# Seventh product of a unit added into the bank that VectorE has just read, instead of into a copy of it

## The chip, the cores and the metric

The kernel runs on one core of one Trainium2 chip. The metric is the device time of one execution in microseconds; lower is better.

## The reference

The reference mixes two results per token with a gate: an attention with a compressive memory over four segments, and a gated feed-forward network. The change lies in the feed-forward half; S = 2048 tokens, D = 576, F = 4608.

```
def _B_ref(x, w_gate, w_up, w_down):
    g = _silu(x @ w_gate)
    u = x @ w_up
    return (g * u) @ w_down
x = A_x
g = sigmoid((x * gate_w).sum(-1, keepdims=True))
a = _A_ref(x, A_wq, A_wk, A_wv, A_wo, A_beta)     # 32 heads, softmax within 4 segments of 512, memory M, z between them
b = _B_ref(x, B_w_gate, B_w_up, B_w_down)
return g * a + (1 - g) * b
```

## The kernel before, in words

The program has three stretches. The first makes the projections of the attention. The last makes the output projection and mixes. Between them, from about 222 to 1634 us, lies the long stretch in which the feed-forward network is computed and the attention runs in its gaps. The change is in this stretch.

**Units.** The 2048 tokens are taken in two halves of 1024, and the 4608 inner features in 36 blocks of 128, so there are 72 units. A unit computes, for one block f and one half, two blocks of 512 tokens of both `x @ w_gate` and `x @ w_up`. That is a product of 2x2 blocks, and it is done with seven block products instead of eight (the sums of weights and of tokens that it needs are made ahead of time). Each operand is split into a high and a low part, so a block product, `seven(t, j)`, is seven matmuls of 128 x 512 into one PSUM bank: six at L1018 and a last one at L1021, which takes the remaining 64 rows of D. With `first=False` a product is added to what the bank holds already.

**The order in a unit** is written out by hand. In it, `a`, `xx` and `y` are PSUM banks (0, 1 and 2), `p5`, `sg0` and `sg1` are rows in SBUF. Products are counted 0 to 6.

| line | engine | what it does |
|---|---|---|
| L1079 | TensorE | product 0 into `a` |
| L1080 | ScalarE | copy of `a` into `xx` |
| L1082, L1083 | TensorE, ScalarE | product 1 into `y`, copied to `p5` |
| L1085, L1087 | TensorE, VectorE | product 2 added in `a`; `y = a + p5` |
| L1089, L1090 | TensorE, ScalarE | product 3 added in `xx`, copied to `sg0` |
| L1092 | TensorE | product 4 added in `a` |
| L1094 | ScalarE | copy of `a` into `xx` |
| L1095 | VectorE | `p5 = a + p5` |
| L1097 | ScalarE | silu of `sg0` |
| L1098, L1099 | TensorE, ScalarE | product 5 added in `y`, silu of it to `sg1` |
| L1102 | TensorE | product 6 added in `xx` |
| L1103, L1104 | VectorE | `sg0 = xx * sg0`, `sg1 = p5 * sg1` |

**What runs between the products.** After each product stands a `tick()`, which calls `beat`. It starts whatever is due by a list of delayed steps: ScalarE's high parts and VectorE's low parts of the next unit's weights (L268, L271), of this unit's results (L962, L963; in some units L136, L137), GpSimd's sums, loads and stores. It then puts groups of the down product (nine matmuls of L868, summed by VectorE at L878) in place, two or three at each tick from the third on, if there are any. Groups come due once in three units, in the unit that follows a full set of three blocks. Then it may advance the attention by a step. A step can hold score matmuls (L726), VectorE's row minimum of the masked scores (L732), ScalarE's exponential (L744), VectorE's and GpSimd's split of it (L758, L759) and the product with the values (L774, L775, summed by VectorE at L781). In units without groups the attention rests at the three ticks after product 5 and 6, so that product 6 follows product 5 directly.

All engines work through their queues in the order in which these lines are issued. The order of accesses to a PSUM bank is kept by semaphores, which the framework sets by tile; all uses of a bank number are uses of one tile.

The bank of a tile is chosen where the helper is made:

```
a_tile = banks(0)
x_tile = banks(1)
y_tile = banks(2)
```

Of the kernel before, what the change touches and what calls it, by code (L numbers as in the profile page):

```python
# [16 lines left out]
AF = mybir.ActivationFunctionType  # L17
# [49 lines left out]
def gated_mix(ctx, tc, xT, xrest, wf, wfr, wfh, wd, wv, wo, beta, cmask, ident, bmask, out):  # L67
    nc = tc.nc
# [31 lines left out]
    def banks(*ids):  # L100
        turn = cycle(ids)
        return lambda shape=(P, L): ps.tile(list(shape), F32, name=f"bank{next(turn)}")
# [4 lines left out]
    first_tile = banks(0, 1, 2, 3, 4)  # L107
    lone_tile = banks(7)
    v_tile = banks(5, 6, 7, 4, 0, 5, 6, 7, *8 * (5, 6, 7))
    a_tile = banks(0)  # L110
    x_tile = banks(1)
    y_tile = banks(2)
    taken = {}
    clock = [0]
# [120 lines left out]
    def r_block(h, o):  # L235
        i, c = divmod(h, 2)
        a, t = (rp.tile([P, 7, 64], d, name=z, bufs=1) for d, z in ((F32, "rr"), (F32R, "rt")))

        def sums():
            nc.gpsimd.tensor_sub(a[:, 5], a[:, 0], a[:, 1])  # L240
            nc.gpsimd.tensor_add(a[:, 1], a[:, 1], a[:, 3])
            nc.gpsimd.tensor_sub(a[:, 4], a[:, 1], a[:, 0])
            nc.gpsimd.tensor_sub(a[:, 6], a[:, 2], a[:, 4])

        def keep(k):
            d = rc[i, 32 * k:32 * k + 32].rearrange("r f (j n) -> (r f) j n", n=P)
            nc.sync.dma_start(d[:, :, 64 * c:64 * c + 64], f32(t))

        return [(o, lambda: nc.sync.dma_start(a[:, 0:4], wfh[h - 4])), (o + 2, sums),
                (o + 3, lambda: nc.scalar.activation(t, a, AF.Copy)), (o + 3, lambda: keep(0)), (o + 3, lambda: keep(1)),  # L250
                (o + 4, lambda: nc.vector.tensor_sub(t, a, f32(t))), (o + 5, lambda: keep(2))]

    def r_fetch(f):
        nc.sync.dma_start(f32(rhs[f % 2][:96]).rearrange("p j n -> p (j n)"), rc[f // 4, :, f % 4])
# [33 lines left out]
    with ExitStack() as st:  # L288
# [188 lines left out]
        for kt in range(NT):  # L477
            if kt % 2 == 0:
                both = staging(), staging()
            a = both[0][:, L * (kt % 2):L * (kt % 2) + 3 * P].rearrange("p (m n) -> p m n", n=P)  # L480
# [209 lines left out]
    with ExitStack() as st:  # L690
# [12 lines left out]
        def row_tile():  # L703
            return rw.tile([P, L], F32, name="row")

        def w_fetch(f):
            ops = wops[1, f] = [None] * 7

            def one(j):
                ops[j] = op_tile()  # L710
                nc.sync.dma_start(f32(ops[j]).rearrange("p a k n -> p (a k n)"), wc[f, j])

            return [(j + 2 if f else FIRST[j], lambda j=j: one(j)) for j in range(7)]
# [219 lines left out]
        def c_tr(o, me):  # L933
            if me is not None:
                nc.gpsimd.tensor_add(o[:, 0:D], o[:, 0:D], me)
            nc.gpsimd.tensor_copy(o[:, 576:640], o[:, 512:576])
            ta = half_tile([P, 4, P])
            for k in range(4):
                nc.tensor.transpose(ta[:, k], o[:, P * k:P * k + P], idt)
            tb = lone_tile([P, P])  # L940
            nc.tensor.transpose(tb, o[:, 512:640], idt)
            oh = cps[0].tile([P, 4, P], F32R, name="oh")
            ol = cps[0].tile([P, 4, P], F32R, name="ol")
            os_ = cps[0].tile([P, P], F32R, name="os")
            split(oh, ol, ta)
            xs_split(os_, tb)
            r = []
            for k in range(4):
                r += [oh[:, k], ol[:, k], oh[:, k]]
            return r + [os_, os_]  # L950
# [31 lines left out]
        def feed(half, f):  # L982
            return [(f // CH, i, hf, hs, ds, yas[half], half) for i in range(8) for hf in range(2)]
# [29 lines left out]
        def seven(t, j, first=True):  # L1013
            w, x = ops[j], XO[j]
            n = 0
            for z in range(2):
                for p, q in ((0, 0), (0, 1), (1, 0)):
                    nc.tensor.matmul(t, w[:, p, z], x[z][:, q], start=first and n == 0, stop=False,  # L1018
                                     skip_group_check=True)
                    n += 1  # L1020
            nc.tensor.matmul(t, rem[:, RPOS[j]], XR[j], start=False, stop=True, skip_group_check=True)  # L1021
# [7 lines left out]
        for pos, (half, f) in enumerate(seq):  # L1029
            if f == 0:  # L1030
                yas[half] = yp.tile([P, 8, D], F32, name="ya")
            q = f % CH
            nxt = seq[pos + 1] if pos + 1 < len(seq) else None
            if q == 0 and f:
                groups += feed(half, f - 1)
                fed.append(f)
            plan = []
            if not nxt:
                plan.append((3, lambda: early.append(c_tr(*tiles.pop(0)))))
            if nxt:  # L1040
                plan += w_fetch(nxt[1]) if nxt[0] and nxt[1] < KEPT else w_make(*nxt)
                if nxt != (0, 1):
                    plan.append((1 if nxt[1] else 10, lambda f=nxt[1]: r_fetch(f)))
                for n, h in enumerate(BLOCKS.get(pos, ())):
                    plan += r_block(h, 4 * n)
                if f + 2 < FT:
                    wraw_of[f + 2] = [None, None]
                    for u in range(2):
                        plan.append(((2, 5)[u] if f or not half else 5 + u, lambda u=u, f=f: wraw_of[f + 2].__setitem__(u, w_load(f + 2, u))))
            if pos == FT - 2:  # L1050
                X2, XR2 = [[None, None] for _ in range(7)], [None] * 7
                plan += [(o + 8, fn) for o, fn in x_second(X2, XR2)]
            for o, fn in plan:
                defer(o + 1, fn)
            step = [0]

            def tick():
                k = step[0]
                step[0] += 1
                if k % 2 == 0 and f and stores:  # L1060
                    nc.sync.dma_start(*stores.pop(0))
                if half == 0:
                    if (q, k) in ((0, 3), (1, 3), (2, 2)):
                        draw[f] = d_load(f)
                    if (q, k) in ((1, 1), (1, 7), (2, 4)):
                        g = f - 1 if k == 1 else f
                        ds[half, g] = d_split(g, draw.pop(g))
                elif (q, k) in ((1, 0), (1, 2), (2, 1)):
                    g = f - 1 if k == 0 else f
                    ds[half, g] = d_fetch(g)  # L1070
                beat(k, half)

            ops, rem = wops.pop((half, f)), rhs[f % 2]
            hh = fp.tile([P, 2, L], F32R, name="hh")
            hl = fp.tile([P, 2, L], F32R, name="hl")
            hs[half, f] = hh, hl
            a, y, xx = a_tile(), y_tile(), x_tile()
            p5, sg0, sg1 = (row_tile() for _ in range(3))
            seven(a, 0)  # L1079
            nc.scalar.activation(xx, a, AF.Copy)  # L1080
            tick()
            seven(y, 1)  # L1082
            nc.scalar.activation(p5, y, AF.Copy)  # L1083
            tick()
            seven(a, 2, False)  # L1085
            y = y_tile()
            nc.vector.tensor_add(y, a, p5)  # L1087
            tick()
            seven(xx, 3, False)  # L1089
            nc.scalar.activation(sg0, xx, AF.Copy)  # L1090
            tick()
            seven(a, 4, False)  # L1092
            xx = x_tile()
            nc.scalar.activation(xx, a, AF.Copy)  # L1094
            nc.vector.tensor_add(p5, a, p5)  # L1095
            tick()
            nc.scalar.activation(sg0, sg0, AF.Silu)  # L1097
            seven(y, 5, False)  # L1098
            nc.scalar.activation(sg1, y, AF.Silu)  # L1099
            tick()  # L1100
            tick()
            seven(xx, 6, False)  # L1102
            nc.vector.tensor_mul(sg0, xx, sg0)  # L1103
            nc.vector.tensor_mul(sg1, p5, sg1)  # L1104
            if q == CH - 1:
                defer(2, lambda t=(hh[:, 0], hl[:, 0], sg0): split(*t))
            else:
                split_by(2, hh[:, 0], hl[:, 0], sg0)
            split_by(3, hh[:, 1], hl[:, 1], sg1)
            tick()  # L1110
            assert not groups
            if f == FT - 1:
                groups += feed(half, f)
                if half == 0:
                    for n in range(BREAK):
                        beat(None if n > 1 else n)
                        if n == 0:
                            down_parts([groups.pop(0) for _ in range(3)], CH - 1, CH)
                    XO, XR = X2, XR2
                    assert not groups  # L1120
# [98 lines left out]
```

## Time and profile before

| | us |
|---|---|
| median of 3 runs | 1725.83 |
| lowest, highest | 1724.3, 1725.91 |
| the profiled execution, its own time | 1724.43 |
| its span | 1722.7 |

| engine | busy, us | instructions |
|---|---|---|
| TensorE, matmul | 1706.5 | 11868 |
| VectorE | 1359.8 | 3231 |
| ScalarE | 1084.8 | 2123 |
| GpSimd | 938.4 | 1194 |

A row of the timeline gives the start, the duration, the engine, the line, the operation, what is written and read, and how often; in brackets how long the engine stood idle before it, and what ended that. A row of waits reads: who waited, for whom, us in total, times, longest. A row of groups gives the count, the busy time and the mean ns of one, then the idle time of the engine just before such instructions and what ended it. PE is TensorE's matmul, PEld its loading of weights, DVE is VectorE, ACT ScalarE, POOL GpSimd, SP the queue that issues transfers.

### The profile page before, as it was taken

Reading aid. Unit: us, or ns where it says so; the run is one execution under the profiler, and the core shown is the slowest. Engines: PE = TensorE matmul, PEld = TensorE weight load, DVE = VectorE, ACT = ScalarE, POOL = GpSimd, SP = SyncE. Lnnn points to the kernel's source line nnn. Section 1 sums busy time; section 2 is a strip of 40 time slices with the busy share of each in tenths; the row PEclk is TensorE's granted clock in tenths of the full one; section 3 lists DMA queues with packets and bytes.
Section 4 is the critical chain, followed back from the end, with each engine's and each line's share of the span. In section 5 each row is a group of like instructions: output and inputs, shape, how many; then the busy total and the mean of one; then the engine's idle time right before and its main releaser. Section 6 shows DMA issues by size and latency. Waiting matters only on the chain.

```text
span 1722.7 us, 34832 instructions
## 1 busy us (share of the span) xinstructions
PE 1706.5 (99%) x11868; PEld 1481.0 (86%) x11868; DVE 1359.8 (79%) x3231; ACT 1084.8 (63%) x2123; POOL 938.4 (54%) x1194
## 2 busy tenths in 40 slices
PE   9999999999999999999999999999999999999999
PEld 7899978888888888888887888888888888888899
DVE  6557588898899889898989677788887778778655
ACT  7666585776677577667765755765666576566411
POOL 4434646666666656565666555555555555555221
PEclk9999999999999999999999999999999999999999
DMA  8654499999998898988879986887778677767544
GB/s 284 233 186 153 151 311 191 232 226 186 209 227 192 181 215 200 193 198 203 210 144 256 290 177 133 178 186 162 148 181 182 147 157 185 163 132 167 165 144 137
DMA packets 524002, 328.05 MB, mean 190 GB/s; under 512 B 411184, under 2 KB 460336, under 8 KB 523824
## 3 DMA queue, kind: packets, MB, share of 16 engines
q1 hardware_dynamic: 523824, 325.83, 77.5%
q8 instruction: 93, 1.52, 0.4%
q14 instruction: 85, 0.70, 0.1%
HBM read 165.76 MB, written 76.09 MB: 140 GB/s over the span
## 4 chain that ended last, share of the span: by engine, by line
PE 83%; DVE 6%; ACT 5%; DMA 3%; issue 2%; POOL 1%; SPq 1%; DVEq 0%; ACTq 0%; POOLq 0%
PE bank L1018 33%; PE bank L868 24%; PE bank L159 10%; PE bank L1021 5%; PE bank L726 4%; PE bank L774 2%; PE bank L775 1%; PE bank L414 1%; ACT pe L744 1%; ACT L744 1%; PE bank L460 1%; DVE xo L137 1%; DVE p L758 1%; DVE scr L732 1%; PE bank L350 1%
## 5 line engine op out<-in xcount | busy, mean ns | idle before, releaser
L759 POOL TENSOR_TENSOR p<-pe,p 128x512 f16<-128x512 f32 x320 | 376.0, 1175 | 420.4 <-DVE p L758 406.2
L868 PE MATMUL bank<-dw,hh 128*128 128x320 f32 (+1 forms) x2304 | 489.0, 305 | 2.8 <-DVE ya L878 2.8
L868 PEld LDWEIGHTS bank<-dw,hh 128*128 128x128 f32 x2304 | 381.4, 190 | 14.4 <-DVE ya L878 3.8
L744 ACT ACTIVATE pe<-bank,mb 128x512 f32<-128x512 f32 (+3 forms) x512 | 247.9, 526 | 197.7 <-DVE mb L732 191.3
L868 PE MATMUL bank<-dw,hl 128*128 128x320 f32 (+1 forms) x1152 | 340.6, 296 | 0.2 <-DVE hl L137 0.2
L732 DVE CUSTOM_DVE_ANT_0 scr<-bank,cm 128x512 bf16<-128x512 f32 (+3 forms) x512 | 246.6, 482 | 6.8 <-PE bank L726 0.2
L878 DVE TENSOR_TENSOR ya<-bank,ya 128x320 f32<-128x320 f32 x352 | 158.3, 453 | 83.9 <-PE bank L868 83.2
L868 PEld LDWEIGHTS bank<-dw,hl 128*128 128x128 f32 x1152 | 218.0, 189 | 0.4 <-DVE hl L137 0.4
L1021 PE MATMUL bank<-xr,rh 128*128 128x512 f32 x504 | 196.5, 390 | 0.0
L752 POOL TENSOR_SCALAR_AFFINE_SELECT pe<-pe 128x256 f32<-128x256 f32 (+1 forms) x320 | 149.8, 469 | 54.1 <-ACT pe L744 51.0
L758 DVE CAST p<-pe 128x512 f16<-128x512 f32 x320 | 152.5, 477 | 0.0
L264 POOL TENSOR_TENSOR ws<-raw 128x256 f32<-128x256 f32 x140 | 118.3, 845 | 17.4 <-DMA raw<-in_wf_dram 4.5
L726 PE MATMUL bank<-kst,qst 108*128 108x512 bf16 (+3 forms) x512 | 125.2, 306 | 2.1 <-ACT pe L744 2.1
L1021 PEld LDWEIGHTS bank<-xr,rh 128*128 128x128 f32 x504 | 94.7, 188 | 20.3
L963 DVE TENSOR_TENSOR hl<-row,hh 128x512 fp32r<-128x512 f32 x120 | 104.2, 868 | 8.3 <-ACT hh L962 7.8
L1095 DVE TENSOR_TENSOR row<-bank,row 128x512 f32<-128x512 f32 x72 | 49.7, 690 | 64.7 <-ACT bank L1094 64.5
L744 ACT ACT_TABLE_LOAD x69 | 88.5, 1283 | 11.1 <-DVE mb L732 10.1
L1080 ACT ACTIVATE bank<-bank 128x512 f32<-128x512 f32 x72 | 41.9, 582 | 80.5 <-PE bank L1021 77.4
L1090 ACT ACTIVATE row<-bank 128x512 f32<-128x512 f32 x72 | 43.3, 601 | 78.0 <-PE bank L1021 77.8
L1097 ACT ACT_TABLE_LOAD x71 | 91.1, 1283 | 1.3
L264 POOL TENSOR_TENSOR ws<-raw,ws 128x256 f32<-128x256 f32 x70 | 58.3, 833 | 49.4 <-DVE wo__22504 L271 10.9
L159 PE MATMUL bank<-xo,qhi 128*128 128x512 f32 x264 | 83.2, 396 | 0.4 <-ACT vps L399 0.4
(2166 smaller groups left out, 4097.9 us busy)
## 6 DMA issues: line engine op xcount, KB each, us to landing
raw<-in_wf_dram SPq DMA_DIRECT2D x140, 256.0 KB
rh<-rc SPq DMA_DIRECT2D x72, 336.0 KB
dc<-dw SPq DMA_DIRECT2D x36, 576.0 KB
dw<-dc SPq DMA_DIRECT2D x36, 576.0 KB
stk<-q SPq DMA_DIRECT2D x32, 384.0 KB
draw<-in_wd_dram SPq DMA_DIRECT2D x36, 288.0 KB
rc<-rt SPq DMA_DIRECT2D x42, 224.0 KB
vd<-vps SPq DMA_DIRECT2D x8, 912.0 KB
```

What stands on the lines that cost most here:

```text
L159: nc.tensor.matmul(t, st[n], mv[n], start=(n == 0), stop=(n == 13))
L264: (nc.gpsimd.tensor_sub if sub else nc.gpsimd.tensor_add)(src[j], p(), q())
L726: nc.tensor.matmul(t[:, c:c + w], qs[:KR, pr, P * i:P * i + P], ks[:KR, pr, 0:w], start=True, stop=True)
L732: nc.vector.tensor_tensor_reduce(scr[:, :w], t[:, c:c + w], cm[:, L - w:L], -SCALE, 3.0e38, OP.add, OP.min, m[:, k:k + 1])
L744: nc.scalar.activation(pe[:, c:c + w], t[:, c:c + w], AF.Exp, bias=m[:, k:k + 1], scale=SCALE)
L752: nc.gpsimd.affine_select(d, d, pattern=pat, compare_op=OP.is_ge, fill=0.0, base=0, channel_multiplier=1)
L758: nc.vector.tensor_copy(p[:, 0], pe)
L759: nc.gpsimd.tensor_sub(p[:, 1], pe, p[:, 0])
L868: nc.tensor.matmul(ts[m], p, q[:, cs], start=(n == 0), stop=(n == 3 * CH - 1))
L878: nc.vector.tensor_add(ya[:, i, cs], t, ya[:, i, cs])
L1018: nc.tensor.matmul(t, w[:, p, z], x[z][:, q], start=first and n == 0, stop=False, skip_group_check=True)
L1021: nc.tensor.matmul(t, rem[:, RPOS[j]], XR[j], start=False, stop=True, skip_group_check=True)
```

## The change

Product 6 is added in `a`, the bank that holds the sum of products 0, 2 and 4, after VectorE has read it at L1095. The copy of that bank by ScalarE (L1094) is gone, and L1103 reads `a` instead of `xx`. Since `a` is now in use until the end of the unit, the two banks change places by unit: the helper gives banks 0, 1, 1, 0, 0, 1, 1, 0 and so on, so that `a` is bank 0 and `xx` bank 1 in one unit, and the other way round in the next.

```
-    a_tile = banks(0)
-    x_tile = banks(1)
+    ax_tile = banks(0, 1, 1, 0)
...
-            a, y, xx = a_tile(), y_tile(), x_tile()
+            a, y, xx = ax_tile(), y_tile(), ax_tile()
...
             seven(a, 4, False)
-            xx = x_tile()
-            nc.scalar.activation(xx, a, AF.Copy)
             nc.vector.tensor_add(p5, a, p5)
             tick()
             nc.scalar.activation(sg0, sg0, AF.Silu)
...
             nc.scalar.activation(sg1, y, AF.Silu)
             tick()
             tick()
-            seven(xx, 6, False)
-            nc.vector.tensor_mul(sg0, xx, sg0)
+            seven(a, 6, False)
+            nc.vector.tensor_mul(sg0, a, sg0)
             nc.vector.tensor_mul(sg1, p5, sg1)
```

## The prediction

> **What bounds the kernel now.** I read the page first: who is busy, and is there anything to win on the busiest engine?
>
> ```profile
> span 1722.7 us, 34832 instructions
> PE 1706.5 (99%) x11868; PEld 1481.0 (86%) x11868; DVE 1359.8 (79%) x3231; ACT 1084.8 (63%) x2123; POOL 938.4 (54%) x1194
> ```
>
> TensorE is filled to 99%; no matmul is added or removed. So the change can only move the moments in which TensorE stands still. The view of waits says which these are, and the rows of VectorE and ScalarE say who waits around the edited lines:
>
> ```profile
> PE bank L1018 <- ACT bank L1094: 3.6, 6, 1.4
> PE bank L868 <- DVE ya L878: 2.8, 4, 0.9
> PE bank L726 <- ACT pe L744: 2.1, 6, 0.4
> PE bank L1018 <- DVE bank L1087: 1.1, 2, 0.7
> PEld bank L1018 <- ACT bank L1094: 8.0, 11, 1.9
> DVE row L1095 <- ACT bank L1094: 64.5, 57, 2.8
> DVE row L1103 <- PE bank L1021: 25.4, 40, 1.9
> DVE row L1103 <- ACT row L1097: 3.1, 5, 0.9
> DVE bank L1087 <- PE bank L1021: 12.5, 21, 1.6
> DVE bank L1087 <- ACT row L1083: 11.4, 12, 1.8
> ACT bank L1094 <- PE bank L1021: 64.0, 44, 3.3
> ```
>
> The columns are total us, times, longest. TensorE's largest wait is exactly for the copy that the change deletes (L1094, first row; the weight loader's row, 8.0, is its upper bound). But the sixth row warns: VectorE's sum L1095, which becomes the new releaser of the seventh product, today starts after that copy, 57 times of 72. Rows of groups by form give the sizes (the third is for a rival further down):
>
> ```profile
> L1094 ACT ACTIVATE bank<-bank 128x512 f32<-128x512 f32 x72 | 42.2, 587 | 64.4 <-PE bank L1021 64.0
> L1095 DVE TENSOR_TENSOR row<-bank,row 128x512 f32<-128x512 f32 x72 | 49.7, 690 | 64.7 <-ACT bank L1094 64.5
> L758 DVE CAST p<-pe 128x512 f16<-128x512 f32 x320 | 152.5, 477 | 0.0
> ```
>
> **The change, part by part.** *Removed: 72 copies of 587 ns, 42.2 us of ScalarE.* ScalarE is idle 37% of the span and stood idle 64.0 us in front of this very copy, so its 42.2 us bring TensorE nothing by themselves. What comes back is the stall in front of the seventh product. I count the products 0 to 6, as the code does: the result of product 4 is copied (L1094) and summed (L1095), product 5 lies between, and product 6 waits. Each product is six matmuls of L1018 and one of L1021. Its stall is the distance from the start of product 5's last matmul to the start of product 6's first one, less the 0.23 us by which such matmuls follow each other when nothing stops them (844.55 to 844.78 in the second of these timelines). The first unit shows a stall; the first two rows are the last matmuls of products 4 and 5:
>
> ```profile
> 229.08 0.39 PE L1021 MATMUL bank<-xr,rh 128*128 128x512 f32 x1
> 230.67 0.39 PE L1021 MATMUL bank<-xr,rh 128*128 128x512 f32 x1
> 231.87 0.50 PE L1018 MATMUL bank<-xo,wo__2681 128*128 128x512 f32 x1 [0.81 <-ACT bank L1094]
> 231.24 0.58 ACT L1094 ACTIVATE bank<-bank 128x512 f32<-128x512 f32 x1
> 230.03 0.08 DVE L732 DVE_READ_ACCUMULATOR2_ANT mb<- 128x1 f32 x1
> 231.85 0.69 DVE L1095 TENSOR_TENSOR row<-bank,row 128x512 f32<-128x512 f32 x1 [1.74 <-ACT bank L1094]
> ```
>
> Stall: 231.87 - 230.67 - 0.23 = 0.97 us; the copy ended at 231.82 and the matmul started 0.05 later. Done for all 72 units from the same rows, the stall shows in ten units: 0.97, 0.49, 0.06, 0.55, 0.23, 0.50, 0.21, 0.51, 0.05 and 1.60, together **5.2 us**. That all goes.
>
> *Added: product 6 waits for L1095.* Its matmuls now write the bank that L1095 reads. Behind the waiting matmul TensorE has product 6, the down products, the attention steps and the next unit in its queue, and VectorE's own L1103 waits for product 6; so the wait is paid in full. So the question is when L1095 would end without the copy ahead of it: as soon as product 4 is done and VectorE is through with what is queued before it, plus 0.69. In the first unit VectorE was through at 230.11 and product 4 ended at 229.47 (229.08 + 0.39), so L1095 would end by about 230.8, before TensorE is ready at 230.90: the 0.97 is won there. It is otherwise where VectorE is the late one:
>
> ```profile
> 844.55 0.39 PE L1021 MATMUL bank<-xr,rh 128*128 128x512 f32 x1
> 844.78 0.39 PE L1018 MATMUL bank<-xo,wo__11789 128*128 128x512 f32 x1
> 843.43 0.58 ACT L1094 ACTIVATE bank<-bank 128x512 f32<-128x512 f32 x1 [1.76 <-PE bank L1021]
> 842.32 1.39 DVE L758 CAST p<-pe 128x512 f16<-128x512 f32 x1
> 843.63 0.62 DVE L781 TENSOR_REDUCE acc<-bank 128x152 f32<-128x456 f32 x1
> 844.17 0.68 DVE L732 CUSTOM_DVE_ANT_0 scr<-bank,cm 128x512 bf16<-128x512 f32 x1
> 844.78 0.68 DVE L1095 TENSOR_TENSOR row<-bank,row 128x512 f32<-128x512 f32 x1
> ```
>
> Here the copy was done at 844.01 and TensorE went on at 844.78 without a pause; VectorE, without one idle moment, got to L1095 only at 844.78 and ended it at 845.46. With the change TensorE waits for it: 845.46 + 0.05 - 844.78 = 0.73 us, out of nothing. The first and the last unit of this kind:
>
> ```profile
> 243.67 0.39 PE L1021 MATMUL bank<-xr,rh 128*128 128x512 f32 x1
> 244.39 0.50 PE L1018 MATMUL bank<-xo,wo__2816 128*128 128x512 f32 x1 [0.33 <-ACT bank L1094]
> 244.37 0.69 DVE L1095 TENSOR_TENSOR row<-bank,row 128x512 f32<-128x512 f32 x1
> ...
> 1628.65 0.39 PE L1021 MATMUL bank<-xr,rh 128*128 128x512 f32 x1
> 1630.47 1.65 PE L1018 MATMUL bank<-xo,wo__22927 128*128 128x512 f32 x6 [1.43 <-ACT bank L1094]
> 1630.52 0.29 DVE L171 TENSOR_TENSOR os<-bank,os 64x128 fp32r<-64x128 f32 x1
> 1630.84 0.69 DVE L1095 TENSOR_TENSOR row<-bank,row 128x512 f32<-128x512 f32 x1
> ```
>
> 243.67 + 0.23 = 243.90 is when TensorE is ready; L1095 ends at 245.06; 245.06 + 0.05 - 243.90 = 1.2 us instead of 0.49. In the last unit 1631.53 + 0.05 - 1628.88 = 2.7 instead of 1.60. Where L1095 had waited for the copy I put its end at 0.61 after the end of VectorE's instruction before it (such instructions overlap by some 0.08, as at 844.78). Over the 72 units fifteen have a stall: 1.22, 0.41, 0.58, 1.07, 0.50, 0.28, 0.87, 0.26, 0.12, 0.13, 0.59, 0.73, 0.12, 0.50, 2.71, together **10.1 us**. All fifteen are units in which no groups of down products are due, so that only product 5, 1.6 us (229.08 to 230.67), separates product 4 from product 6. In the 22 units with such groups whole groups of nine matmuls stand between, and none of them stalls.
>
> *Is L1095 really free of the copy?* Both only read the bank, so no data goes from one to the other; the 57 waits are there because two engines are kept off one bank. The Trainium skill's page PSUM — Partial Sum Buffer, section "PSUM bank collisions raise a hardware error", says so: accesses of different engines to one bank must be ordered, reads against reads too. By that rule the order disappears with the copy, as I reckon, and the trace agrees with its 64.5 us. If the wait came from something that stays, L1095 would keep its present end: product 6 would then stall in 34 units for 18.0 us by the same working, 12.8 more than now. I take 10.1 because nothing in the code but the copy orders the two.
>
> *What is moved: the banks change places.* The first product of the next unit goes to the bank that L1090 read last, some three products earlier, instead of the one that L1095 read; neither is awaited in any row of TensorE above. ScalarE's copy L1080 overwrites the bank that L1103 reads, as before. I cost this at nothing; its cover is the two or three products of 1.6 us each between; without it each unit would stall by a read of 0.6 us. No DMA and no queue of SP or GpSimd is passed.
>
> *Relief.* VectorE loses 64.5 us of waiting. For TensorE that counts only if it lasts until L1095 of the next unit. It mostly doesn't: VectorE falls back into step with TensorE at L1103 (40 of 72) and at L1087 (33 of 72 by the two rows). Where it runs through, three or four units, 0.1 to 0.6 us each can be saved; I take 0.5 us in all, with 0 and 1.2 as the bounds. The other three TensorE rows (2.8, 2.1, 1.1) hang on L878, L744 and L1087, which lie elsewhere in the unit; I leave them.
>
> **Sum:** -5.2 + 10.1 - 0.5 = +4.4 us. The profiled execution took 1724.43 us (span 1722.7 and 1.7 around it): 1728.8. Two of the three timed runs lie at 1725.8 and 1725.9, so the median, 1725.83, is 1.4 above the profiled one; I forecast **1730.2 us** for the median. A measurement of this kernel tells about 0.2% (3.5 us) from no change; 4.4 us is 0.25%.
>
> **Rivals.** *Faster: VectorE's freed time carries over.* The mean wait that goes is 64.5 / 57 = 1.13 us. If VectorE reached L1095 1.1 us earlier in the fifteen units, only the last one and a trace of the second would be left of the list, 1.7 us; the balance is -3.5, about 1722.3, and with all stalls gone 1720.6. From 0.4 us on it breaks even (the list less 0.4 each leaves 5.2). For it: without the copy ScalarE reaches the gate's L1097 earlier, for which L1103 waits 3.1 us, 5 times. Against it stands the falling into step named above. A unit with 1.07 us in the list shows how:
>
> ```profile
> 431.76 0.70 DVE L1087 TENSOR_TENSOR bank<-bank,row 128x512 f32<-128x512 f32 x1 [0.50 <-ACT row L1083]
> ```
>
> VectorE was idle at L1087, so whatever it had gained before is lost there; what makes it late comes after, in the same unit, and doesn't move. Chance 0.16.
>
> *No change that shows.* The same mechanism at about half strength: VectorE 0.2 to 0.5 us earlier leaves 7.3 to 4.3 us of stalls, -0.9 to +2.1 us, 1725 to 1728. For it: the forecast lies close to the bound. Chance 0.22.
>
> *Far slower: VectorE becomes the bound of these units.* Its instructions stretch (the cast at 842.32 took 1.39 us where its mean is 477 ns) when other engines shift. If it came one operation of 0.69 us later in each unit without groups, the fifteen stalls would grow by 10.4 and those units that are now less than 0.7 us early would add some 3.5: about +18 us, 1744. Or the order against the copy has another cause: +12.8, 1738. Against both: the rows around L1095 don't depend on the copy. Chance 0.10.
>
> **How the numbers follow.** The forecast, 0.52: stalls between 8 and 13 us, 1727.5 to 1734; nine tenths of it lie over 0.2%. Slower: 0.52 x 0.9 + 0.10 = 0.57, with the upper edge of the middle case 0.60. Same 0.24. Faster 0.16. The range reaches down into the faster case, to 1722, and up to the unfavourable order, 1737; the ends of the two outer cases are left out.
>
> **What would show it.** In the changed profile TensorE's row "L1018 <- ACT L1094" must be gone and a row that names VectorE's sum of L1095 stand in its place, with 10 to 16 waits, the longest in the last unit; VectorE's 64.5 us must be gone, and its idle time at L1103 larger. ScalarE must have 72 ACTIVATEs and 42 us less. The first unit must be faster by about a microsecond and the unit at 844 slower by 0.7. I am wrong if the new row is under 5 us (VectorE gained more than I gave it) or if a new wait stands at product 0 or at L1080 (the exchange of banks).

## The result and the profile after

The changed kernel takes 1730.44 us (median of 7 runs, 1729.02 to 1733.13) against 1725.05 (7 runs, 1724.3 to 1725.91). The ratio is 1.0032, with a 95% interval of 1.0022 to 1.0041: slower by 5.4 us. Lines behind the edit move up by one to three: the seven products are L1017 and L1020 now, VectorE's sum is L1092, its product L1100.

The first lines of the page and the rows of waits that answer to those shown before (who waited, for whom, us in total, times, longest):

```profile
span 1728.7 us, 34789 instructions
PE 1707.4 (99%) x11868; PEld 1480.9 (86%) x11868; DVE 1362.6 (79%) x3231; ACT 1048.8 (61%) x2051; POOL 939.7 (54%) x1194
```

```profile
PE bank L1017 <- DVE row L1092: 7.5, 10, 2.1
PE bank L867 <- DVE ya L877: 2.8, 4, 0.9
PE bank L725 <- ACT pe L743: 2.1, 6, 0.4
PE bank L1017 <- DVE bank L1086: 0.7, 1, 0.7
...
DVE row L1100 <- PE bank L1020: 40.3, 48, 2.6
DVE row L1092 <- PE bank L1020: 29.1, 35, 2.1
```

ScalarE has lost the 72 copies, and TensorE has gained nothing by that: ScalarE's busy time fell by 36 us, its share from 63% to 61%. The largest wait of TensorE has changed hands, from ScalarE's copy (3.6 us) to VectorE's sum (7.5 us). VectorE's sum no longer waits for the copy; it waits for TensorE instead, 29.1 us, and the product that needs product 6 waits 40.3 us (25.4 before). Of TensorE's other rows two stand as they were, and the one for VectorE's `y` (L1086, before L1087) fell from 1.1 to 0.7.

Three units of the timeline, for the reader to lay beside the prediction's: the first, the second, the last. The first row of each is the last matmul of product 5, the second the first of product 6, and the last row is the sum. In the last unit two low parts of VectorE stand before it:

```profile
231.48 0.39 PE L1020 MATMUL bank<-xr,rh 128*128 128x512 f32 x1
231.71 1.07 PE L1017 MATMUL bank<-xo,wo__2681 128*128 128x512 f32 x4
230.67 0.69 DVE L1092 TENSOR_TENSOR row<-bank,row 128x512 f32<-128x512 f32 x1
...
243.37 0.39 PE L1020 MATMUL bank<-xr,rh 128*128 128x512 f32 x1
244.99 1.39 PE L1017 MATMUL bank<-xo,wo__2814 128*128 128x512 f32 x5 [1.23 <-DVE row L1092]
244.16 0.69 DVE L1092 TENSOR_TENSOR row<-bank,row 128x512 f32<-128x512 f32 x1
...
1633.29 0.39 PE L1020 MATMUL bank<-xr,rh 128*128 128x512 f32 x1
1635.78 1.63 PE L1017 MATMUL bank<-xo,wo__22785 128*128 128x512 f32 x6 [2.10 <-DVE row L1092]
1633.89 0.69 DVE L136 TENSOR_TENSOR ol<-bank,oh 128x512 fp32r<-128x512 f32 x1 [2.49 <-ACT oh L135]
1634.62 0.29 DVE L170 TENSOR_TENSOR os<-bank,os 64x128 fp32r<-64x128 f32 x1
1634.94 0.69 DVE L1092 TENSOR_TENSOR row<-bank,row 128x512 f32<-128x512 f32 x1
```

In the first unit VectorE is early and the stall of 0.97 us is gone (231.71 - 231.48 is the usual distance). In the second unit VectorE runs through and ends the sum at 244.85; TensorE has been ready since 243.60 and waits 1.39 us, where it had waited 0.49 for the copy. In the last unit it is 2.26 instead of 1.60: the sum stands behind two low parts of the output stage (L136, L170). These come late because VectorE stood idle for 2.49 us ahead of L136, waiting for ScalarE's high part (L135).

Measured over all 72 units in the way of the prediction (distance of starts less the usual 0.23), product 6 stalls 15 times for **10.9 us**, where before it was 10 times for 5.2. (The row of waits above has 10 times and 7.5 us for the same thing: it counts from the modelled end of the matmul before, which lies 0.16 us later than the moment at which TensorE would be ready, and it puts some of these waits down to another engine.) At product 4 the stalls fell from 2.2 us (5 units) to 1.2 (2 units). All other stalls together rose by 1.2. That gives +5.9; the spans differ by 6.0 (1728.7 - 1722.7), the medians by 5.4.

### The profile page after: what moved, and what is told of

It reads as the page before. It is cut to its first block, busy times and chain, and to the rows that moved or that the text cites. A ratio compares the mean times of both kernels' runs of the same rounds, so it can differ in the third digit from the quotient of the medians.

```text
span 1728.7 us, 34789 instructions
## 1 busy us (share of the span) xinstructions
PE 1707.4 (99%) x11868; PEld 1480.9 (86%) x11868; DVE 1362.6 (79%) x3231; ACT 1048.8 (61%) x2051; POOL 939.7 (54%) x1194
## 4 chain that ended last, share of the span: by engine, by line
PE 81%; DVE 7%; ACT 3%; DMA 3%; issue 2%; SPq 1%; POOL 1%; DVEq 0%; POOLq 0%; ACTq 0%
PE bank L1017 32%; PE bank L867 23%; PE bank L158 11%; PE bank L1020 5%; PE bank L725 4%; PE bank L773 2%; PE bank L774 1%; PE bank L459 1%; PE bank L413 1%; DVE p L757 1%; DVE scr L731 1%; DVE hl L962 1%; ACT L743 1%; ACT pe L743 1%; DMA xo<-in_xT_dram 1%
## 5 line engine op out<-in xcount | busy, mean ns | idle before, releaser
L1020 PE MATMUL bank<-xr,rh 128*128 128x512 f32 x504 | 196.4, 390 | 0.0
L1020 PEld LDWEIGHTS bank<-xr,rh 128*128 128x128 f32 x504 | 94.6, 188 | 20.4
L1100 DVE TENSOR_TENSOR row<-bank,row 128x512 f32<-128x512 f32 x72 | 49.6, 689 | 49.0 <-PE bank L1020 40.3
L373 POOL TENSOR_TENSOR q<-qr,q 128x512 bf16<-128x512 f32 x36 | 44.4, 1233 | 71.1 <-ACT q L372 62.3
```

## Experiments

The theory: TensorE waits at product 6 for VectorE's sum, and the price is how late VectorE comes to that sum in its queue. The rivals: the exchange of banks costs the time; the missing copy costs it through ScalarE's order; VectorE's load, not its order, is the bound. Stalls are given by the measure just used. Each ratio is to the kernel before, run on the same chip.

**1. Without the exchange of banks.**

```
-    ax_tile = banks(0, 1, 1, 0)
+    ax_tile = banks(0, 1)
```

> The change without the exchange of banks: a is bank 0 and xx bank 1 in every unit. My theory (product 6 waits for VectorE's sum of the bank, and the exchange costs nothing): product 0 of the next unit now writes the bank that VectorE's product sg0 = a * sg0 still reads. In the changed kernel's profile that instruction ends after TensorE is ready for the next unit's product 0 in 48 units, by 58 us in all. So about 1730 + 58 less what VectorE catches up meanwhile (0 to 11 us of the stalls at product 6): 1777 to 1788, with a new row of TensorE waiting for that product. Rival (the exchange itself costs the 5 us, because product 0 or the first copy of the unit waits on the other bank): back to about 1725.

Measured: 1793.87 us, ratio 1.0398 (1.0384 to 1.0413).

```profile
PE bank L1017 <- DVE row L1100: 49.1, 48, 2.3
PE bank L1017 <- DVE row L1092: 5.3, 8, 1.1
```

A new row stands on top: product 0 of the next unit waits for VectorE's L1100, in 48 units. These are the 50 units without down products less the last one of each half. By the distances it is 56.8 us in 48 units, where the working on the trace had said 58 in 48. The stalls at product 6 fell only from 10.9 to 8.3, and the stalls between the matmuls inside product 0 rose by 5.6 (2.4 to 7.9), most of it because after a stalled first matmul the second came 0.11 us later than usual. That is why the total is 6 us above the expected range. The exchange is no cost; without it the change would have lost 69 us. Its cover, which the prediction named and priced at 0.6 us a unit, is real, and its price is 1.2 us a unit (56.8 / 48), since VectorE has to get to the instruction as well as to do it.

**2. The copy put back, unused.** Product 6 is still added in `a`; `xx` gets a copy that nobody reads.

```
             seven(a, 4, False)
+            nc.scalar.activation(xx, a, AF.Copy)
             nc.vector.tensor_add(p5, a, p5)
```

> The change with ScalarE's copy of the bank put back in its old place, into xx, where nothing reads it; product 6 is still added in a. My theory: the copy and VectorE's sum are kept apart only because both read one bank, so VectorE's sum starts after the copy again, as before, and product 6 waits for it: by the working on the trace of before, 34 units stall for 18 us instead of 15 for 10 to 11, so about 1737 to 1738, and the row of VectorE waiting for the copy is back at about 60 us. Rival 1 (the loss comes from the missing copy, by another order on ScalarE): about 1725, as before. Rival 2 (VectorE's backlog alone sets product 6, the copy makes no difference to it): 1730 as the change.

Measured: 1741.47 us, ratio 1.0093 (1.0079 to 1.0106).

```profile
PE bank L1017 <- DVE row L1093: 14.0, 17, 2.5
DVE row L1093 <- ACT bank L1092: 65.9, 57, 2.8
```

The wait of the sum for the copy is back, 57 times for 65.9 us (before: 57 times, 64.5), although no data goes from one to the other. Product 6 stalls in 32 units for 17.6 us; the prediction's unfavourable bound had been 34 and 18.0. Both rivals fall: with the copy on ScalarE the kernel isn't back at 1725, and the copy makes a difference to the sum. The total is some 4 us above the expected value; 2.5 of this stands between the matmuls inside product 6, whose stalls went from 4.2 to 6.7, and the rest isn't traced.

**3. The sum ahead of a block of background work.** The tick after product 3 goes behind product 4 and the sum; nothing is added or left out.

```
-            tick()
             seven(a, 4, False)
             nc.vector.tensor_add(p5, a, p5)
             tick()
+            tick()
```

> The change with one block of background work (the tick after product 3) moved behind product 4 and VectorE's sum: VectorE reaches the sum without that block's instructions ahead of it, and TensorE has that block's work between products 4 and 6. Nothing is added or left out. My theory: the stalls of 10.9 us at product 6 nearly vanish (0 to 2 us left); new stalls of about 1.4 us in 4 units appear at product 4, which now follows product 3 directly and needs the bank that VectorE reads for y. So 1730.4 - 10.9 + 1 to 4 = 1721 to 1724, below the kernel before. Rival (VectorE is the bound in these units by its load, so wherever the sum stands the wait comes back at another product): 1728 to 1731, with the stalls at product 4 or 5 instead.

Measured: 1719.95 us, ratio 0.9968 (0.9956 to 0.998). It beats the kernel before by 5.2 us and the changed one by 10.5.

```profile
PE bank L725 <- ACT pe L743: 2.8, 7, 0.7
PE bank L867 <- DVE ya L877: 2.8, 4, 0.9
PE bank L1017 <- DVE bank L1086: 1.7, 4, 0.7
...
DVE row L1091 <- PE bank L1020: 51.1, 52, 2.5
```

No row of product 6 is left, and by the distances it doesn't stall once. Product 4 stalls in 6 units for 2.6 us, since it follows product 3 directly; 1.4 more than in the changed kernel, as expected. VectorE now stands ready and waits for product 4 in 52 units (51.1 us; 29.1 in 35 in the changed kernel). With the same load on VectorE no wait of that size came back elsewhere, so the load is not the bound.

**4. The same move in the kernel before,** with the copy and the sum both ahead of the block.

```
-            tick()
             seven(a, 4, False)
             xx = x_tile()
             nc.scalar.activation(xx, a, AF.Copy)
             nc.vector.tensor_add(p5, a, p5)
             tick()
+            tick()
```

> The kernel before with the same move: the block of background work after product 3 goes behind product 4, the copy and the sum. My theory: the copy is then ahead of that block's ScalarE work, its stalls of 5.2 us at product 6 go, 1.4 us at product 4 come: 1720 to 1723, about as fast as the change with the same move. Rival (load, not order): no change, 1725.

Measured: 1732.18 us, ratio 1.004 (1.0028 to 1.0053). I was wrong here. The stalls at product 6 went, all 5.2 us of them, as expected. But others came in many places: product 4 stalls in 13 units for 4.9 us (5 for 2.2 before), product 1 in 3 units for 1.6, the attention's matmuls of L726 and L774 5.3 us more in all, and the stalls inside products 0 and 5 rose by 1.7 and 2.8, while those inside products 4 and 6 fell by 2.1 and 1.0.

```profile
PE bank L726 <- ACT pe L744: 4.3, 9, 0.9
PE bank L1018 <- DVE bank L1087: 2.9, 7, 0.7
PE bank L868 <- DVE ya L878: 2.8, 4, 0.9
PE bank L774 <- ACT pe L744: 1.9, 2, 1.1
...
DVE row L1094 <- ACT bank L1093: 88.9, 67, 3.1
ACT bank L1093 <- PE bank L1021: 66.6, 71, 1.3
```

The last two rows hint at why: the copy (now L1093) waits for product 4 in 71 of 72 units, 44 before, with the block's exponentials (L744) behind it in ScalarE's queue; and VectorE's sum waits for the copy 88.9 us instead of 64.5, with the block's casts and row minima behind it.

**5. The sum ahead, the copy behind the block,** to test that reading.

```
-            tick()
             seven(a, 4, False)
             xx = x_tile()
-            nc.scalar.activation(xx, a, AF.Copy)
             nc.vector.tensor_add(p5, a, p5)
             tick()
+            nc.scalar.activation(xx, a, AF.Copy)
+            tick()
```

> The kernel before with the sum moved ahead of the block of background work, but the copy put behind that block on ScalarE, for the question why the move made the kernel with the copy slower (1732). Theory A: there the copy, which waits for product 4, stood in ScalarE's queue ahead of the block's exponentials and held the attention up; behind the block it holds nothing up, and the time is 1720 to 1724, near the change with the same move (1720). Theory B: the copy costs because of ScalarE's load or because it keeps VectorE's sum off the bank, wherever it stands: 1728 to 1733.

Measured: 1730.45 us, ratio 1.0028 (1.0017 to 1.004), in the range of theory B.

```profile
PE bank L1018 <- ACT bank L1095: 5.1, 9, 1.6
PE bank L1018 <- DVE bank L1087: 1.4, 3, 0.7
...
ACT bank L1095 <- DVE row L1093: 43.1, 49, 2.1
DVE row L1103 <- ACT row L1097: 16.1, 20, 2.1
```

The scattered waits of experiment 4 are mostly gone (product 4: 6 units, 2.4 us), as theory A said. But the copy is the late one now: it waits for VectorE's sum (43.1 us, 49 times, the two reads of the bank have merely changed order), and product 6 waits for it, 19 times for 7.2 us by the distances. VectorE's product L1103 waits 16.1 us (3.1 before) for the silu L1097, which stands behind the copy on ScalarE. So the copy costs at either place, each time by another wait. What the 12 us between experiments 3 and 4 consist of, piece by piece, stays open; what is shown is that, of the forms tried, the move pays only without the copy. Theory B's two causes, ScalarE's load and the bank, are not told apart.

**6 and 7. One more VectorE instruction ahead of the sum,** in the changed kernel and in the kernel before. Its result is not used.

```
+            nc.vector.tensor_mul(sg1, p5, p5)
             nc.vector.tensor_add(p5, a, p5)
```

> The change with one more VectorE instruction of 128 x 512 (about 0.68 us, its result is not used) just ahead of the sum in each of the 72 units. My theory (product 6 waits for the sum, so VectorE's lateness at that place is paid by TensorE): with 0.68 us put in front of the sum in the changed kernel's profile, 31 units stall for 24.6 us in place of 15 for 10.9, so about 1744, and all of it at product 6. Rival (VectorE's load in general is what costs): the same rise here as in the kernel before with the same instruction. Rival 2 (the cost lies elsewhere, VectorE has room): 1730 to 1732.

> The kernel before with the same VectorE instruction ahead of its sum. My theory: product 6 waits there for ScalarE's copy alone, so the sum may be late; 0 to +3 us, 1725 to 1728, what there is coming from products or down products that wait for later VectorE work. Rival (VectorE's load): the same rise as in the changed kernel, about +14 us, 1739.

Measured: 1767.33 us in the changed kernel (ratio 1.0249, 1.0235 to 1.0264), which is 37 us more than without it; 1736.94 in the kernel before (1.0069, 1.0055 to 1.0082), 12 more. Both are larger than expected; first the size. From the view of one line, in the changed kernel:

```profile
L1092 DVE TENSOR_TENSOR row<-row x72: 677/773/1659, 231.0 to 1667.9; 128x512 f32<-128x512 f32 x72
```

(shortest, median, longest, in ns), and as rows of groups, the added instruction and the sum behind it:

```profile
L1092 DVE TENSOR_TENSOR row<-row 128x512 f32<-128x512 f32 x72 | 65.4, 909 | 0.0
L1093 DVE TENSOR_TENSOR row<-bank,row 128x512 f32<-128x512 f32 x72 | 49.8, 692 | 13.9 <-PE bank L1020 8.0 <-DVE row L1092 0.5
```

I had counted on 680; the mean is 909, and the sum starts 0.10 behind it. With 1.01 us in front of the sum, the working on the changed kernel's trace gives 36.0 us of stalls at product 6 in 38 units. Measured: 41.0 in 41. So 30 of the 37 us stand where the theory puts them, ahead of product 6, and 3 more between its own matmuls:

```profile
PE bank L1017 <- DVE row L1093: 30.3, 31, 2.7
```

and the same instruction in the kernel before leaves product 6 alone:

```profile
PE bank L1018 <- ACT bank L1094: 3.8, 7, 1.2
PE bank L1018 <- DVE wo__10235 L271: 1.0, 1, 1.0
PE bank L1018 <- DVE wo__3708 L271: 1.0, 1, 1.0
```

(10 units and 5.3 us there, 10 and 5.2 before). Of the 12 us that it costs all the same, 8.5 are stalls between the matmuls of a product, 8.3 of them inside product 0; the two rows for weights' low parts (L271), which come late, point at them. So VectorE's load is not free there. How much of the 37 us it would explain doesn't follow from this pair: in the kernel before, VectorE's wait for the copy fell from 64.5 to 25.6 us, so much of the added time went into idle time. In the changed kernel the stalls inside product 0 didn't move (2.4 us).

**8 and 9. The moved block in two parts.** In the units without down products, only the delayed steps of the block after product 3 go behind the sum (8), or only the attention's step (9). In the first, TensorE's order is the changed kernel's in all units but the last, where five transposes of the output stage (0.46 us), one of the delayed steps, go behind product 4 as well. Kernel 8:

```
+            held = []
+            if due and not groups:
+                held, due[0] = due[0], []
             tick()
             seven(a, 4, False)
             nc.vector.tensor_add(p5, a, p5)
+            for fn in held:
+                fn()
             tick()
```

Kernel 9:

```
-            tick()
+            if groups:
+                tick()
+            else:
+                for fn in due.popleft() if due else ():
+                    fn()
+                due.appendleft([])
             seven(a, 4, False)
             nc.vector.tensor_add(p5, a, p5)
+            if step[0] == 3:
+                tick()
             tick()
```

> The change; of the background block after product 3 only the delayed steps (low and high parts of weights and results) go behind the sum, in the units without down products; the attention's step stays ahead, so TensorE's order is the same and no matmul more stands between products 4 and 6. It parts the two effects of the move. Theory A (what counts is VectorE's queue ahead of the sum): about 0.4 to 1 us of VectorE's work leaves the queue ahead, which by the list of stalls leaves 2 to 6 of the 10.9 us: 1721 to 1726. Theory B (the move helped because TensorE has more work between products 4 and 6): no change, 1730.

> The change; of the same block only the attention's step goes behind the sum in the units without down products, the delayed steps stay ahead. One to 2 us of VectorE's row minima and casts leave the queue ahead, and 0.1 to 1.1 us of TensorE's work go between products 4 and 6. Theory A and B both: stalls at product 6 of 0 to 1.5 us, 1719 to 1722. If it stays above 1726, the attention's step is not what makes VectorE late.

Measured: 1722.25 us for 8 (ratio 0.9982, 0.9974 to 0.9991), 1726.07 for 9 (0.9998, 0.9989 to 1.0007). Stalls at product 6: 2.9 us in 5 units for 8, 5.0 in 8 units for 9. Of kernel 8, waits and the unit that I had followed at 844 us:

```profile
PE bank L1017 <- DVE row L1095: 2.1, 5, 0.8
PE bank L1017 <- DVE bank L1086: 0.7, 1, 0.7
```

```profile
843.34 0.68 DVE L1095 TENSOR_TENSOR row<-bank,row 128x512 f32<-128x512 f32 x1
843.95 1.14 DVE L270 TENSOR_TENSOR wo__11727<-raw,wo__11727 128x256 fp32r<-128x256 f32 x1
...
844.43 0.39 PE L1020 MATMUL bank<-xr,rh 128*128 128x512 f32 x1
844.66 1.68 PE L1017 MATMUL bank<-xo,wo__11727 128*128 128x512 f32 x6
```

The same work in the changed kernel:

```profile
845.87 0.41 DVE L270 TENSOR_TENSOR wo__11727<-raw,wo__11727 128x256 fp32r<-128x256 f32 x1
846.21 1.39 DVE L757 CAST p<-pe 128x512 f16<-128x512 f32 x1
...
848.67 0.68 DVE L1092 TENSOR_TENSOR row<-bank,row 128x512 f32<-128x512 f32 x1
```

The low part L270 that stood ahead of the sum runs behind it now, and product 6 starts 0.23 us behind the last matmul of product 5. In this unit the sum starts 1.31 us sooner after `y` is made (L1086); about 1 us of that is the cast, which took 0.41 us here instead of 1.39. In thirteen others of the fifteen units that had stalled, the instructions between `y` and the sum are the same but for one low part, and the sum starts 0.33 to 0.75 us sooner. In the last unit it is 3.4 us, since the two low parts that waited for ScalarE are behind it too. In these 71 units kernel 8 has no matmul more between products 4 and 6, and yet two thirds of their stalls are gone (8.6 us, now 2.9); the last unit's 2.3 us are gone too. So VectorE's queue ahead of the sum is what counts (theory A), not cover on TensorE. Kernel 9 missed my 0 to 1.5 us:

```profile
PE bank L1017 <- DVE row L1097: 3.0, 4, 1.8
```

With the delayed steps still ahead of it the sum is late in 8 units, the last one (2.0 us) among them, where the attention is over and the delayed steps alone make the sum late; and product 4 stalls in 5 units for 2.4 us, as in experiment 3. The time stands on the mark of 1726 above which I would have given up the attention's step as a cause; the stalls at product 6, which fell from 10.9 to 5.0, say that the step is a part of it.

## Why the prediction was right

**The stall that goes.** 5.2 us at product 6 for ScalarE's copy. TensorE's row for it is gone, and the first unit won its microsecond. ScalarE has 72 instructions less, and their durations add up to 41 us less, as foreseen; its busy time fell by 36 alone, because the copies had overlapped with their neighbours and busy time counts an overlap once.

**The stall that comes.** 10.1 us in fifteen units was worked out; 10.9 us in fifteen units was measured. Fourteen are the same units. Their stalls, in order of time: 1.39, 0.25, 0.67, 1.13, 0.60, 0.33, 0.95, 0.33, 0.21, 0.67, 0.82, 0.20, 0.60, 0.47 and 2.26; the 0.47 is new, and one foreseen at 0.13 did not come. The unit at 844 us, foreseen at 0.73, is the one of 0.82. The list could be read off the trace of before because VectorE's lateness arises, in most of these units, out of work that the edit does not touch. In nine of the fifteen VectorE was idle at `y` (L1086) in the same unit; in four it was last idle at the product L1100 of the unit before. Whatever it had gained was lost there, as the prediction had argued. In the last unit the lateness is not of VectorE's making: it waited for ScalarE's high part. Experiments 3 and 8 take work away from in front of the sum, and the stalls go, all of them in 3 and 8.0 of 10.9 us in 8; 6 adds work there, and they grow.

**The freed order.** That two reads of one bank are kept apart, and that this order would vanish with the copy, was argued then and is shown by experiment 2: the copy alone brings back 57 waits and takes the stalls to 17.6 us. The Trainium skill's rule (PSUM — Partial Sum Buffer, "PSUM bank collisions raise a hardware error") agrees with it.

**The exchange of banks at nothing.** Right as a part of this change (no stall at product 0 in the changed kernel). The price without the cover was mis-sized: 0.6 us a unit said, 1.2 measured.

**The relief and the release.** -0.5 us was taken for VectorE's freed time, at product 6. Product 6 came out 0.8 above the list, and three things make that up: a later release, a relief and the new stall of 0.47. The prediction let TensorE start 0.05 us behind the sum, as it had behind the copy. In all fifteen stalls it starts 0.15 behind (in the second unit from 244.85 to 244.99), which makes about 1.3 us over the fourteen units of the list. By the records of the trace the first weight load of product 6 now waits for two semaphores, one that VectorE raises (it has the sum) and one that ScalarE raises (it writes the weights' high parts), and one of them is waited for by an instruction of its own of 0.05 us. The view of the line of the products counts these, first in the kernel before, then in the changed one (shortest, median, longest, in ns):

```profile
L1018 PEldq EVENT_SEMAPHORE  x15: 51/51/51, 218.8 to 964.3; - x15
L1017 PEldq EVENT_SEMAPHORE  x63: 51/51/51, 219.4 to 1635.7; - x63
```

In experiment 2, where there are 15 as before, the same sum is followed after 0.05 us. The prediction had no term for this. No run takes the second semaphore alone away, so that it is the cause is read from these records and not shown by itself. Against it stands a relief of about 1.0 us in three units (foreseen at 0.41, 0.13 and 2.71), twice the term of 0.5 and within its bounds. Another 1.0 us was saved at product 4, which the prediction had left alone, and 1.2 us of other small differences came on top. So +4.4 became +5.9 by the distances and +5.4 in the medians. That it came so close is partly luck: these errors cancel in part, and the forecast of 1730.2 met 1730.44 also because the median before, over more runs, came out 0.8 lower.

**The rivals.** VectorE's freed 64.5 us did not carry over: 69.4 us of waiting for TensorE stand at the sum and at the product now (29.1 + 40.3), 25.4 before. At half strength 4.3 to 7.3 us of stalls should have been left, and it was 10.9. VectorE did not become the bound: its instructions did not stretch (1359.8 us busy before, 1362.6 now). The unfavourable order did not come by itself, and was built in experiment 2.

## What to carry to other kernels

When a copy is removed and a consumer waits for another reader of the same bank instead, the price is not the reader's duration (0.69 us here) but its place in its engine's queue: line up, unit by unit, when the new releaser ends and when the waiting engine is ready, and sum only the positive differences. Look also at how many engines the waiting instruction then waits for: here TensorE started 0.15 us behind its releaser in place of 0.05. If those differences come from work that happens to be issued ahead of the releaser, move that work behind it before giving up the edit: here this turned a loss of 5.4 us into a gain of 5.2. Exchange banks by unit when one is now held to the end of the unit; without it product 0 of the next unit stalled in 48 units, for 57 us in all.

## What the runs showed of the hardware

A VectorE product of two SBUF rows of 128 x 512, added 72 times, took between 677 and 1659 ns with a mean of 909, while the sum of the same size behind it, which reads one operand from PSUM, had a mean of 692 (experiment 6). So an added instruction of that kind can't be counted on as a delay of a known size.

The first matmul of product 6 started 0.15 us behind VectorE's sum where its weight load waited for two semaphores (the changed kernel), and 0.05 us behind it where it waited for one (experiment 2).
